# The maximum over the keys as a ScalarE copy and three two-operand maxima, normalised rows on ScalarE, and new core orders in a two-layer attention and SSM kernel

## The chip, the cores and the metric

The kernel runs on one core of a Trainium2 chip. Its engines each work through their own instruction queue in order: TensorE (PE in the profile; PEld is its weight load), VectorE (DVE), ScalarE (ACT), GpSimd (POOL), and SyncE (SP), whose queue issues the DMAs here. Semaphores let one queue wait for another. The metric is the device time of one execution in microseconds; before the change it was 403.94 us (median of three runs, 403.01 to 404.91).

## The reference

Two kinds of layer alternate, A, B, A, B, each added to its input after a layer norm. x has 2048 rows of 512 bfloat16 values.

```python
def _A_ref(x, wqkv, wo):            # H = 32 heads of Dh = 16; W, dil = 8, 2
    qkv = (x @ wqkv).reshape(B, S, 3, H, Dh) ...
    idx = pos[:, None] - off[None, :]            # 8 keys: the row itself and 2, 4, .. 14 rows back
    kg, vg = k[:, :, idx_c, :], v[:, :, idx_c, :]
    logits = jnp.einsum("bhsd,bhswd->bhsw", q, kg) * scale
    logits = jnp.where(mask, logits, -1e9)
    attn = softmax(logits, axis=-1)              # over the 8 keys
    o = jnp.einsum("bhsw,bhswd->bhsd", attn, vg)
    return o.reshape(B, S, D) @ wo

def _B_ref(u, ...):                 # a long convolution of each of the 512 columns with a kernel K
    ...                             # K from a sum over 128 complex modes; rfft, product, irfft
    return y + u * Dskip

x = x + _A_ref(layernorm(x), ...);  x = x + _B_ref(layernorm(x), ...)
x = x + _A_ref(layernorm(x), ...);  x = x + _B_ref(layernorm(x), ...)
```

A softmax is the same whatever is subtracted from all eight logits of a row, so the maximum need not be exact.

## The kernel before

The program is one stream of five stages: generation of the convolution kernels together with the front of attention layer 0 (up to about 108 us of the span), the core of attention layer 0 (to about 190 us), the first convolution as a chain of DFT matmuls together with the front of layer 1 (to about 266 us), the core of attention layer 1 (to about 356 us), and the second convolution (to the end). Inside a stage the order of every engine's queue is written by hand: a string of letters is walked, and each letter issues the instructions of one step. An engine takes its own instructions of these steps in the order of the string, so that a letter's place decides what stands ahead of it in each queue.

The rows are split so that row `16p + a` lies on partition `p` in block `a`; a core handles 16 blocks `a`, four of them to a group `q`. The steps of a core (`LayerA.core`) and their letters:

- `q`, `v` (lines 390 to 408): projections for the queries of one group and a quarter of the features, and for the values of one block. Four matmuls on PE, then an evacuation of PSUM by ACT. The last value blocks of even and of odd number start a DMA that shifts values between partitions.
- `m` (line 342): the products of queries and keys for one group and a quarter of the features, one DVE instruction of 128x4096; there are two buffers for them, so the second next `m` waits until PE has read the first.
- `l` (lines 350, 354): PE sums these products over the 16 features of a head, into the logits `L` of the group, 128x1024 float32 in PSUM. For the first two groups of a core `L` is laid out as (head, block) by key by row, for the other two as row by block by key by head.
- `x` (`mx`, line 414): DVE takes the maximum over the eight keys, from PSUM, as one `tensor_reduce` with 1024 elements in and 128 out, bfloat16.
- `e` (`sub_exp`, lines 425, 426): PE subtracts the maximum within PSUM with a negated identity matrix, then ACT takes the exponential.
- `r`, `n`, `T`: PE sums the exponentials, ACT forms the reciprocal by Ln and Exp, DVE multiplies (lines 445, 448), and for the first two groups PE and ACT turn the weights to rows (`T`).
- `P` (line 467): DVE multiplies the weights of one block with its eight value rows, 128x4096, into `pav`, of which there are two buffers.
- `S`, `V` (lines 482 to 494): PE sums `pav` over the keys and turns it, into the PSUM tile `po`, of which there is one; ACT evacuates it to `oT`. `S` and `V` take the blocks in the order in which `P` made them.
- `O` (lines 501 to 510): PE adds x and projects with `wo`; ACT writes `x_sb`, for blocks below 12 with the row sum, and squares it for the second sum.
- `b`, `d`, then `a` or `f`: the statistics of four blocks, and the normalised input of the convolution, one block of 128x512 at a time, on DVE (`a`, line 197) or on ACT (`f`, line 195). Both letters take the next block from one list of twelve; core 0 does eight of them there and leaves the others to POOL.
- Core 0 also holds work of the convolution to come: `0` and `2` to `5` make a table of sines on POOL and ACT, `1` and `6` issue loads, `8` and `9` add a row, `A` to `H` copy parts of the kernel to `k_perm` (line 1450; `B`, `C`, `E` on ACT, the others on DVE), `w` loads a matrix.

After core 0 the string `ORDER0` begins with `KD KA KA KA KD`: first DFT matmuls of the convolution kernels (line 802), their PSUM evacuated by DVE (`D`) or ACT (`A`) on line 791. After core 1 `ORDER1` begins with the same step for the normalised rows, so that it needs all twelve blocks and the last four.

Two lines set memory that the change touches. In layer 0 a tile `gap` keeps room free ahead of the work tiles:

```python
            if l == 0:
                wk.tile([P, 1680], BF16, name="gap", bufs=1)
```

Of the kernel before, what the change touches and what calls it, by code (L numbers as in the profile page):

```python
# [11 lines left out]
ALU = mybir.AluOpType  # L12
AX = mybir.AxisListType
PSUM = bass.MemoryType.PSUM
F32 = mybir.dt.float32
BF16 = mybir.dt.bfloat16
# [4 lines left out]
P = 128  # L21
# [4 lines left out]
W = 8  # L26
# [23 lines left out]
zUUUkkzkUztKkKtkkTUpexUUKUEkUkeUkUKpKUokxkpxpKUkUxxkqUKEpxoqkkUpUUxopXXXKQpZxxZZ  # L50
"""
ORDER0 = """
KD KA KA KA KD KA KD KA KD KA KD kA KA kD KA KD UA KD UA UA UD KA kA kD kA UD
UA UD UA kD kA kD u UD u u UA m m m UA u u UD u UA m kD UA kD UA m
m u UA u m kA u kD u m kD u kD kA kA yA m YA m yD u yA u m m m
u u yA m m u YA m yA w000D yD yA YD yA w010D YA yD yA
"""
LATE0 = "a s t g r b m"
ORDERF = """
yA h00 YA h01 v100A v110D h10 a0 z12A p0 z11A n0D h11 w001A w011A S a1 p1 T0 E01A z13A E00D n1G H2  # L60
P02 a2 P00 Q00 p2 T1 E10D E11D P01 P11 P12 n2D H3 a3 P13 T2 P10 E20D E21D P03 p3 P21 P22 n3D
P23 T3 E30D E31A P20 x1
"""
ORDER1 = """
UA UD UA UD UA UA UD UA UD UD u u m m u u m m UA u UA UD m UA u u
UD UA u m m u u m m u YD m u YA YA m u yD m yA u u m m u w001A
m m yA yA w000D YA yD yA YD w011D yA yD w010D yA yD yA v101A v103D v113A v102D v112D v111D v110A v100A
"""

CORE0 = """  # L70
vmvvvlmqlxmvvvemlvqrlmqvnTmlvxqqlmevlrvmmvvvvnPllPqxmSqTeO0mPlVrP15SOS2PnOPVPOSml4qOOlb3mV78lPPC
SOdxS6eOrPSPPOSnwaOPSBPOSaOS9bOfAPdbFPOtVftEGDSaafaOH
"""
CORE1 = """
0m1l2ml3mvvqlmvlvqmxmqvlqqvemllvmrqvlnmTmqxqlmvvelvvvvmPvPqvrlnlTqSmOSxmPqlPeSPOmSOSlOPrlSOqPSPO
SnmPOOlbxSOPePVbPrdSnPdfOVfaOPwSfPOSfOSbafOPdfaSttfaOa
"""
ROWS0 = (0, 2, 1, 3, 4, 5, 6, 7, 8, 9, 10, 11, 12, 13, 14, 15)
ROWS1 = (0, 2, 1, 3, 4, 5, 6, 7, 8, 9, 10, 11, 12, 13, 14, 15)
# [120 lines left out]
class LayerA:  # L200
# [158 lines left out]
    def core(self, x_sb, u, lnp, order, ev, nprod=0):  # L359

        tc, nc, lnst, l = self.tc, self.nc, self.lnst, self.layer
        ident, nident = self.c["ident"], self.c["nident"]
        scale = float(DH) ** -0.5
        xnT, ncol = self.xnT, self.ncol
        if self.ps_l is None:
            self.open_logits()
        st, linit, mult, lsum = self.st, self.linit, self.mult, self.lsum

        with ExitStack() as c2:
# [6 lines left out]
                self.load_wo(big)  # L376
            wk = c2.enter_context(tc.tile_pool(name=f"a{l}_wk", bufs=2, reuse_waits="tile"))
            if l == 0:
                wk.tile([P, 1680], BF16, name="gap", bufs=1)
            self.prp = c2.enter_context(tc.tile_pool(name=f"a{l}_prod", bufs=2, reuse_waits="tile"))  # L380
            pavp = c2.enter_context(tc.tile_pool(name=f"a{l}_pav", bufs=2, reuse_waits="tile"))
            ps_q = c2.enter_context(tc.tile_pool(name=f"a{l}_ps_q", bufs=2, space=PSUM))
# [27 lines left out]
            def mx(q):  # L410
                L = st[q]["L"]
                m = wk.tile([P, P], BF16, name="mx", bufs=1)[:]
                st[q]["mx"] = m if q < ncol else m.rearrange("p (a h) -> p a h", h=H)
                nc.vector.tensor_reduce(st[q]["mx"], L[:].rearrange("c w p -> c p w" if q < ncol else "p a w h -> p a h w"), AX.X, ALU.max)

            def sub_exp(q):
                L, m = st[q]["L"], st[q]["mx"]
# [120 lines left out]
            def calls(f, *args):  # L538
                return [lambda a=a: f(*a) for a in args]

            def logit(f):
                def g(q, ft):
                    if ft == 0:
                        linit(q)
                    f(q, ft)
                return g
# [5 lines left out]
                m=calls(mult, *qft[nprod:]), l=calls(logit(lsum), *qft[nprod:]),  # L552
                q=calls(q_proj, *qft[len(self.qT) * NDT:]), v=calls(v_proj, *((a,) for a in VROWS)),
                x=calls(mx, *blocks), e=calls(sub_exp, *blocks), r=calls(recip, *blocks), n=calls(norm_p, *blocks), T=calls(turn, *blocks[:ncol]),
                P=calls(pv_mult, *rows), O=calls(out_proj, *rows[:15]), t=calls(x_stats, (12,), (13,)),
                b=calls(u_begin, (0, 4, "act", "pool"), (4, 8, "act", "act"), (8, 12, "act", "act")),
# [1023 lines left out]
```

## Time and profile before

| | before |
|---|---|
| median of three runs | 403.94 us (403.01 to 404.91) |
| span of the profiled execution | 402.6 us, so 1.3 us of the median lie around it |
| busy DVE, PE, ACT, POOL | 95%, 81%, 80%, 15% of the span |
| maximum over the keys (line 414) | 8 instructions, 9.7 us on DVE |
| normalised rows in the cores, on DVE | 13 instructions, 5.1 us (line 197) |
| normalised rows in the cores, on ACT | 11 instructions, 8.9 us (line 195) |

A page of the profile gives the busy time of each engine, the chain of work that ended last, and groups of instructions with their mean duration. Further views are drawn from the same trace: busy time by stretches of the span, the instructions of one engine in order of time, and groups within a stretch. All times are of one execution; "start, duration" pairs of neighbouring instructions overlap a little on one engine, so that the distance from start to start, the step, is what an instruction costs its queue.

### The profile page before, as it was taken

How to read it: one execution, taken by the hardware profiler on the slowest of the kernel's cores; microseconds unless marked ns; L12 is line 12 of the kernel's file. 1: busy time of each engine (PE TensorE's matmuls, PEld its weight loads, DVE VectorE, ACT ScalarE, POOL GpSimd, SP SyncE). 2: the span in 40 equal slices, each digit the busy share in tenths (PEclk: the TensorE clock that was granted, in tenths of full speed). 3: DMA queues.
4: the chain of work that ended last, by engine and by line, in shares of the span. 5: the costliest groups of instructions: out<-in, count | busy, mean ns of one | idle time of the engine just before them, and what ended most of it. 6: DMA issues, size and time to landing. Idle time of an engine off the chain costs nothing.

```text
span 402.6 us, 14781 instructions
## 1 busy us (share of the span) xinstructions
PE 328.0 (81%) x6527; PEld 230.3 (57%) x6527; DVE 383.5 (95%) x460; ACT 321.8 (80%) x557; POOL 59.1 (15%) x75
## 2 busy tenths in 40 slices
PE   3000059999999989999998889999999998997895
PEld 2000026657735656756987888543456666566885
DVE  6999999999999999999999998979899999989994
ACT  7999888898656578988999987674666677989974
POOL 9402400000199500200600000100000001000000
PEclk9999997999999999999999999999999999999999
DMA  7952711115013875259236685730063019504606
GB/s 219 395 143 37 81 52 50 44 27 117 3 43 76 214 210 160 55 173 384 93 112 232 228 285 166 280 114 2 0 170 94 3 39 383 161 2 134 186 14 202
DMA packets 62323, 54.17 MB, mean 135 GB/s; under 512 B 33869, under 2 KB 50738, under 8 KB 60978
## 3 DMA queue, kind: packets, MB, share of 16 engines
q1 hardware_dynamic: 62250, 53.22, 43.5%
q8 instruction: 51, 0.84, 0.9%
q14 instruction: 14, 0.11, 0.1%
q10 hardware_dynamic: 8, 0.00, 0.0%
HBM read 30.15 MB, written 13.24 MB: 108 GB/s over the span
## 4 chain that ended last, share of the span: by engine, by line
PE 36%; DVE 31%; ACT 17%; issue 8%; DMA 5%; SPq 2%; POOL 1%; DVEq 0%; ACTq 0%; POOLq 0%
DVE pav L467 11%; PE pq L398 6%; PE pk L1268 5%; ACT a1s L791 5%; PE pp L1206 4%; DVE t L847 3%; PE pq L223 3%; DVE prod L342 3%; PE pp L282 3%; PE L L350 2%; ACT ub L860 2%; DVE B_t L1110 2%; DVE sq_z L1085 2%; DMA v_ext<-v_ext 2%; DMA kf_ring<-kf_dram 2%
## 5 line engine op out<-in xcount | busy, mean ns | idle before, releaser
L467 DVE TENSOR_TENSOR pav<-attn,v_ext 128x4096 bf16<-128x4096 bf16 (+1 forms) x34 | 72.4, 2168 | 0.4 <-DMA v_ext<-v_ext 0.3
L342 DVE TENSOR_TENSOR prod<-qT,kT_ext 128x4096 bf16<-128x4096 bf16 x29 | 67.0, 2341 | 1.4 <-PE L L350 0.9
L1196 PE MATMUL pt<-ident,x_blk 128*128 128x128 bf16 x64 | 5.9, 241 | 42.8 <-DVE x_blk L197 38.6
L1110 DVE TENSOR_TENSOR A_t<-A_t,pow_t 128x1024 bf16<-128x1024 bf16 (+4 forms) x46 | 38.3, 870 | 0.3
L492 PEld LDWEIGHTS <-pav 64*128 64x128 bf16 x1664 | 26.2, 95 | 13.5 <-DVE pav L467 8.6
L503 PE MATMUL pq<-wop,oT 128*128 128x512 bf16 x128 | 32.9, 379 | 0.7 <-ACT oT L494 0.7
L860 ACT CAST ub<-pb 128x1024 bf16<-128x1024 f32 x32 | 32.1, 1079 | 1.2 <-PE pb L809 1.2
L492 PE MATMUL po<-ident,pav 64*128 64x64 bf16 x1664 | 29.3, 190 | 4.2 <-DVE pav L467 3.2
L400 ACT CAST v_ext<-pq 128x512 bf16<-128x512 f32 x32 | 18.8, 586 | 16.2 <-PE pq L398 16.2
L809 PE MATMUL pb<-a1s,w_sb 128*128 128x64 bf16 x768 | 27.4, 193 | 5.0 <-ACT a1s L791 1.7
L398 PE MATMUL pq<-wv,xnT 128*128 128x512 bf16 x128 | 30.6, 380 | 0.0
L1206 PE MATMUL pp<-xnT,kT_ext 128*128 128x512 bf16 x96 | 27.1, 411 | 4.3 <-ACT kT_ext L1211 2.3
L1196 PEld LDWEIGHTS <-x_blk 128*128 128x128 bf16 x64 | 4.6, 107 | 44.8 <-DVE x_blk L197 38.8
L809 PEld LDWEIGHTS <-w_sb 128*128 128x128 bf16 x768 | 24.9, 98 | 7.2 <-issue 5.2
L791 ACT CAST a1s<-pb 128x1024 bf16<-128x1024 f32 x29 | 28.2, 1059 | 0.8 <-PE pb L802 0.8
L1268 PEld LDWEIGHTS <-A_t 128*64 128x64 bf16 (+1 forms) x512 | 22.9, 107 | 4.5 <-DVE B_t L1110 0.3
L1268 PE MATMUL pk<-B_t,A_t 128*64 128x84 bf16 (+1 forms) x512 | 24.6, 206 | 0.0
L791 DVE CAST a1s<-pb 128x1024 bf16<-128x1024 f32 x19 | 22.6, 1217 | 1.4 <-PE pb L802 1.3
L223 PE MATMUL pq<-xnT,kT_ext 128*128 128x512 bf16 x96 | 23.9, 380 | 0.0
L225 ACT CAST qT<-pq 128x512 bf16<-128x512 f32 x24 | 14.1, 586 | 9.3 <-PE pq L223 9.2
L509 ACT ACTIVATE x_sb<-pq 128x512 bf16<-128x512 f32 x24 | 14.3, 594 | 8.7 <-PE pq L503 8.7
L398 PEld LDWEIGHTS <-xnT 128*128 128x128 bf16 x128 | 11.6, 98 | 15.3 <-issue 3.0
(259 smaller groups left out, 897.0 us busy)
## 6 DMA issues: line engine op xcount, KB each, us to landing
w_sb<-w_dram SPq DMA_DIRECT2D x8, 1024.0 KB, 7.8
w_dram<-xnT SPq DMA_DIRECT2D x1, 4096.0 KB
kf_ring<-kf_dram SPq DMA_DIRECT2D x13, 256.0 KB, 4.8
kf_ring<-kf_dram SPq DMA_DIRECT2D x26, 128.0 KB, 4.3
v_ext<-v_ext SPq DMA_DIRECT2D x4, 784.0 KB, 6.6
x_blk<-in_A_x_dram SPq DMA_DIRECT2D x4, 512.0 KB, 4.1
kT_ext<-in_A_wqkv_dram SPq DMA_DIRECT2D x4, 512.0 KB, 9.2
x_sb<-in_A_x_dram SPq DMA_DIRECT2D x4, 512.0 KB, 5.3
```

The source lines that it names most:

```text
L223: nc.tensor.matmul(pq[:], lhsT=self.wqk[:, dt, ft * P:(ft + 1) * P], rhs=self.xnT[:, dt, q * 512:(q + 1) * 512], start=(dt == 0), stop=(dt ...
L342: nc.vector.tensor_tensor(pr, self.qT[q][:, ft].unsqueeze(1).to_broadcast([P, W, 4, P]), kap, ALU.mult)
L398: nc.tensor.matmul(pp[:], lhsT=xnT[:, dt, a * P:(a + 1) * P], rhs=wv[:, dt, :], start=(dt == 0), stop=(dt == NDT - 1))
L467: nc.vector.tensor_tensor(pv[:, i], attn[:, n % 4].unsqueeze(2).to_broadcast([P, W, DH // parts, H]), vap, ALU.mult)
L492: nc.tensor.matmul(po[:, h, 0, i * nt + ft, :], lhsT=pvf[rows, i, w, ft * P:(ft + 1) * P], rhs=ident[rows, rows], start=(w == 0 and ft + i ...
L503: nc.tensor.matmul(pw[:], lhsT=oT[:, ftp, :], rhs=self.wo[:, ftp, :], start=False, stop=(ftp == NDT - 1))
L791: (self.nc.scalar.copy if eng == "act" else self.nc.vector.tensor_copy)(dst, src)
L809: nc.tensor.matmul(p2[:, j, :], lhsT=self.w2[:, ec * EC + j, :], rhs=a1s[:, ec * EC + j, :], start=True, stop=True)
L860: nc.scalar.copy(ub[:], p2)
L1110: return lambda: nc.vector.tensor_tensor(*args)
L1206: nc.tensor.matmul(pps[kind, b, ft][:], lhsT=la.wqk[:, dt, c:c + P], rhs=la.xnT[:, dt, b * 512:(b + 1) * 512], start=(dt == 0), stop=(dt = ...
L1268: nc.tensor.matmul(o, lhsT=lhs, rhs=Bt[:, ri, c * CH + ql].rearrange("p b g -> p (b g)"), start=(not half and j % 4 == 0 and ri == 0), sto ...
```

## The change

The maximum becomes four instructions: ACT copies `L` from PSUM to a bfloat16 tile `lc` in SBUF, and DVE takes maxima of halves, of 4 keys with 4 (512 elements), of 2 with 2 (256) and of 1 with 1 (128), each on what the one ahead of it wrote. In layer 0 `lc` takes its room from `gap`; in layer 1 it gets a pool of its own on the other side of the memory, where the front's tiles have been closed. The strings of both cores are new; those of the other stages only have their lines broken elsewhere. In core 0 all eight normalised rows are `f` (they were three `f` and five `a`), in core 1 ten are `f` and two `a` (they were seven and five). All other letters occur as often as before.

```diff
 CORE0 = """
-vmvvvlmqlxmvvvemlvqrlmqvnTmlvxqqlmevlrvmmvvvvnPllPqxmSqTeO0mPlVrP15SOS2PnOPVPOSml4qOOlb3mV78lPPC
-SOdxS6eOrPSPPOSnwaOPSBPOSaOS9bOfAPdbFPOtVftEGDSaafaOH
+vvmm0vlxvvlemmvvrlvqqnvlTmqlqmmlxvvlevvrmmnvvvlqPTlSPmxqOVeqm15qll2PPmS4OOSPP3l78m6rVPOSCbOOPnVP
+BlxSPOOdSefwPSrfOPnSOPSfPOSfPOSbOAdffVb9fPODSHGfttEFO
 """
 CORE1 = """
-0m1l2ml3mvvqlmvlvqmxmqvlqqvemllvmrqvlnmTmqxqlmvvelvvvvmPvPqvrlnlTqSmOSxmPqlPeSPOmSOSlOPrlSOqPSPO
-SnmPOOlbxSOPePVbPrdSnPdfOVfaOPwSfPOSfOSbafOPdfaSttfaOa
+0mqq2mlm13lqlvvvmlvmmxvvllqevvmrmnqllqTqqmmlmxvvvvvvvvlPPqmlmeqlSmxrqSqnTPOOSePSPPOSOlPSbOOSPdfr
+flmmSffnPPOOllxSbOPVdPeSrffnPOVOSOPPSOfSwbfPOSdffaattO
 """
...
-                wk.tile([P, 1680], BF16, name="gap", bufs=1)
+                wk.tile([P, 1680 - W * P], BF16, name="gap", bufs=1)
+            lcp = c2.enter_context(tc.tile_pool(name="a1_lc", bufs=1, side="right", reuse_waits="tile")) if l else wk
...
                 st[q]["mx"] = m if q < ncol else m.rearrange("p (a h) -> p a h", h=H)
-                nc.vector.tensor_reduce(st[q]["mx"], L[:].rearrange("c w p -> c p w" if q < ncol else "p a w h -> p a h w"), AX.X, ALU.max)
+                lc = lcp.tile([P, W * P], BF16, name="lc", bufs=1)[:]
+                lc = lc.rearrange("c (w p) -> c w p", w=W) if q < ncol else lc.rearrange("p (a w h) -> p a w h", a=4, w=W)
+                nc.scalar.copy(lc, L[:])
+                for n in (4, 2, 1):
+                    lo, hi = (lc[:, 0:n], lc[:, n:2 * n]) if q < ncol else (lc[:, :, 0:n, :], lc[:, :, n:2 * n, :])
+                    one = st[q]["mx"].unsqueeze(1 if q < ncol else 2)
+                    nc.vector.tensor_tensor(lo if n > 1 else one, lo, hi, ALU.max)
```

More of the change, by code (lines that the diff above doesn't have):

```diff
@@ L52 @@
 ORDER0 = """
[L53 to L56, printed above, removed]
+KD KA KA KA KD KA KD KA KD KA KD kA KA kD KA KD UA KD UA UA UD KA kA kD kA UD UA UD UA kD kA kD u UD
+u u UA m m m UA u u UD u UA m kD UA kD UA m m u UA u m kA u kD u m kD u kD kA kA yA m YA m yD u yA u
+m m m u u yA m m u YA m yA w000D yD yA YD yA w010D YA yD yA
 """
@@ L60 @@
 yA h00 YA h01 v100A v110D h10 a0 z12A p0 z11A n0D h11 w001A w011A S a1 p1 T0 E01A z13A E00D n1G H2
-P02 a2 P00 Q00 p2 T1 E10D E11D P01 P11 P12 n2D H3 a3 P13 T2 P10 E20D E21D P03 p3 P21 P22 n3D
-P23 T3 E30D E31A P20 x1
+P02 a2 P00 Q00 p2 T1 E10D E11D P01 P11 P12 n2D H3 a3 P13 T2 P10 E20D E21D P03 p3 P21 P22 n3D P23 T3
+E30D E31A P20 x1
 """
 ORDER1 = """
-UA UD UA UD UA UA UD UA UD UD u u m m u u m m UA u UA UD m UA u u
-UD UA u m m u u m m u YD m u YA YA m u yD m yA u u m m u w001A
-m m yA yA w000D YA yD yA YD w011D yA yD w010D yA yD yA v101A v103D v113A v102D v112D v111D v110A v100A
+UA UD UA UD UA UA UD UA UD UD u u m m u u m m UA u UA UD m UA u u UD UA u m m u u m m u YD m u YA YA
+m u yD m yA u u m m u w001A m m yA yA w000D YA yD yA YD w011D yA yD w010D yA yD yA v101A v103D v113A
+v102D v112D v111D v110A v100A
 """
 CORE0 = """
-vmvvvlmqlxmvvvemlvqrlmqvnTmlvxqqlmevlrvmmvvvvnPllPqxmSqTeO0mPlVrP15SOS2PnOPVPOSml4qOOlb3mV78lPPC
-SOdxS6eOrPSPPOSnwaOPSBPOSaOS9bOfAPdbFPOtVftEGDSaafaOH
+vvmm0vlxvvlemmvvrlvqqnvlTmqlqmmlxvvlevvrmmnvvvlqPTlSPmxqOVeqm15qll2PPmS4OOSPP3l78m6rVPOSCbOOPnVP
+BlxSPOOdSefwPSrfOPnSOPSfPOSfPOSbOAdffVb9fPODSHGfttEFO
 """
 CORE1 = """
-0m1l2ml3mvvqlmvlvqmxmqvlqqvemllvmrqvlnmTmqxqlmvvelvvvvmPvPqvrlnlTqSmOSxmPqlPeSPOmSOSlOPrlSOqPSPO
-SnmPOOlbxSOPePVbPrdSnPdfOVfaOPwSfPOSfOSbafOPdfaSttfaOa
+0mqq2mlm13lqlvvvmlvmmxvvllqevvmrmnqllqTqqmmlmxvvvvvvvvlPPqmlmeqlSmxrqSqnTPOOSePSPPOSOlPSbOOSPdfr
+flmmSffnPPOOllxSbOPVdPeSrffnPOVOSOPPSOfSwbfPOSdffaattO
 """
```

## The prediction, as put down before the changed kernel had run

> **What bounds the kernel now.** I read the page first: it gives the span and the busy time of each engine.
>
> ```profile
> span 402.6 us, 14781 instructions
> ...
> PE 328.0 (81%) x6527; PEld 230.3 (57%) x6527; DVE 383.5 (95%) x460; ACT 321.8 (80%) x557; POOL 59.1 (15%) x75
> ```
>
> DVE is the fullest engine, but a share over five stages says little, so the next view is busy time by stage (bounds, length, then busy us of PE, PEld, DVE, ACT, POOL): core 0, first convolution, core 1, second convolution, and three stretches inside the cores.
>
> ```profile
> 108.30:190.50 82.20, 78.15 (x1495) 48.25 (x1493) 81.55 (x64) 61.55 (x124) 29.77 (x17) 1.00 0.53 157
> 190.50:265.80 75.30, 69.69 (x1689) 59.36 (x1690) 71.83 (x116) 66.59 (x85) 8.10 (x11) 1.00 0.59 204
> 265.80:356.50 90.70, 87.39 (x1576) 50.15 (x1573) 87.84 (x77) 63.56 (x135) 1.02 (x1) 1.00 0.30 96
> ...
> 167.30:191.10 23.80, 22.42 (x568) 14.63 (x568) 23.38 (x31) 20.45 (x48) 0.00 (x0) 1.00 0.67 237
> 265.80:291.00 25.20, 24.65 (x165) 9.92 (x162) 23.26 (x19) 14.89 (x26) 0.00 (x0) 1.00 0.02 7
> ...
> 351.05:356.50 5.45, 4.80 (x52) 2.19 (x50) 5.22 (x18) 4.84 (x11) 0.00 (x0) 1.00 0.05 16
> ```
>
> In core 0 DVE idles 0.65 of 82.2 us: whatever leaves its queue there should shorten the stage, until another engine sets the pace. ACT has 20.6 us free in core 0 and 27.1 in core 1, but only 3.35 in the last 23.8 us of core 0. In core 1 DVE idles 2.9 us. The groups of DVE within core 1 show on what (last column):
>
> ```profile
> L342 DVE TENSOR_TENSOR prod<-qT,kT_ext 128x4096 bf16<-128x4096 bf16 x16 | 36.2, 2286 | 1.3 <-PE L L350 0.9 <-DVE kT_ext L295 0.2
> L467 DVE TENSOR_TENSOR pav<-attn,v_ext 128x4096 bf16<-128x4096 bf16 (+1 forms) x17 | 36.1, 2160 | 0.4 <-DMA v_ext<-v_ext 0.3
> ```
>
> The chain of waits at the end of core 0 tells who receives the time saved there:
>
> ```profile
> 191.11 0.75 ACT a1s L791
> ...
> 197.94 5.49 ACT a1s L791 x6
> ```
>
> The first convolution begins as a queue of ACT evacuations. A gain of core 0 counts only as far as ACT comes free earlier than 191.11; DVE alone being early is worth nothing there.
>
> **The maximum.** What goes is one reduction for each group of rows, eight in all; what comes on DVE is three dependent maxima of 512, 256 and 128 elements. DVE in order of time:
>
> ```profile
> 18.43 0.42 DVE L1110 TENSOR_TENSOR B_t<-B_t,cm_t 128x512 bf16<-128x512 bf16 x1
> 18.77 0.69 DVE L1082 SCALAR_TENSOR_TENSOR sq_z<-sq_z 128x512 f32<-128x512 f32 x1
> ...
> 27.87 0.28 DVE L1110 TENSOR_TENSOR A_t<-A_t,pow_t 128x256 bf16<-128x256 bf16 x1
> 28.18 0.29 DVE L1110 TENSOR_TENSOR A_t<-A_t,A_t 128x256 bf16<-128x256 bf16 x1
> ...
> 167.32 1.21 DVE L414 TENSOR_REDUCE mx<-L 128x128 bf16<-128x1024 f32 x1
> 168.46 2.27 DVE L467 TENSOR_TENSOR pav<-attn,v_ext 128x4096 bf16<-128x4096 bf16 x1
> ...
> 175.66 0.40 DVE L197 TENSOR_SCALAR xnT<-x_sb,ln_rstd,ln_nb 128x512 bf16<-128x512 bf16 x1
> 175.98 2.27 DVE L467 TENSOR_TENSOR pav<-attn,v_ext 128x4096 bf16<-128x4096 bf16 x1
> ```
>
> The reduction costs its queue 1.14 us (167.32 to 168.46). A follower that is independent starts about 0.08 before the record ends (18.43+0.42 against 18.77), one that reads the result 0.03 after it (27.87+0.28 against 28.18). No row shows a bfloat16 maximum; the nearest are these two-operand instructions, which do multiply, add and subtract at one rate, so I price it as they are: 0.42+0.03, then 0.285+0.03, then 128 elements, by the same slope 0.215, less 0.07 of overlap with an independent follower: 0.92. Saved: 0.22 each, 0.88 in each core. Bounds: if the three did not wait for each other, 0.34+0.20+0.14 = 0.68, saving 0.46 each; if maxima ran like float32 instructions of the same size (18.77: 0.69 at 512, so 0.42 and 0.28 for the halves, again with 0.03, 0.03 and less 0.07), 1.38, a loss of 0.24 each. I take the dependent bfloat16 price.
>
> The Trainium skill, "VectorE: DVE Perf Modes", section "The DRAIN you can't avoid", speaks against splitting: no operation starts until the one ahead has emptied the pipe, so that its rules ask for fewer operations. The rows disagree with the first half (18.77 starts 0.08 before 18.43+0.42 is over). By that rule the reduction would cost its whole 1.21 and the three 0.42+0.28+0.215, a saving of 0.29 each, 2.3 in all against 1.8 by the rows.
>
> On ACT comes a 1024-element copy from PSUM. The exponential reads the same tile in the same shape:
>
> ```profile
> L426 ACT ACTIVATE ex<-L 128x1024 bf16<-128x1024 f32 x8 | 8.2, 1026 | 1.3 <-PE L L425 1.3
> ```
>
> less 0.09 of overlap, 0.93 each, 3.7 in each core. It lies ahead of the maximum, so it must be hidden: in both new strings one to three products or `P` stand on DVE between the last `m` of a group and its `x`, 2.2 us each, against PE's sums, this copy, and at most an evacuation ahead of it. I take no wait; without that cover each group would pay up to 0.93. What queues behind a copy that waits are the evacuations that free PE's two projection buffers.
>
> **The rows.** Five rows in core 0 and three in core 1 leave DVE: 0.32 each (175.66 to 175.98). On ACT they cost 0.71 (188.83 to 189.54), from its own tail in order of time:
>
> ```profile
> 187.41 1.03 ACT L1450 COPY k_perm<-k_rl 128x1024 bf16<-128x1024 bf16 x1
> 188.35 0.58 ACT L494 CAST oT<-po 128x512 bf16<-128x512 f32 x1
> 188.83 0.82 ACT L195 ACTIVATE xnT<-x_sb,ln_nb,ln_rstd 128x512 bf16<-128x512 bf16 x1
> 189.54 0.57 ACT L507 CAST x_sb<-pq 128x512 bf16<-128x512 f32 x1
> 190.54 0.59 ACT L507 CAST x_sb<-pq 128x512 bf16<-128x512 f32 x1 [0.42 <-PE pq L503]
> 191.11 1.01 ACT L791 CAST a1s<-pb 128x1024 bf16<-128x1024 f32 x1
> ```
>
> **The end of core 0.** The last `P` and what follows it on DVE:
>
> ```profile
> 186.05 1.22 DVE L467 TENSOR_TENSOR pav<-attn,v_ext 128x2048 bf16<-128x2048 bf16 x1
> 187.18 1.28 DVE L138 BATCH_NORM_STATS2 ln_bn<-x_sb 128x6 f32<-128x512 bf16 x2
> 188.38 0.75 DVE L1450 COPY k_perm<-k_rl 128x1024 bf16<-128x1024 bf16 x2
> 189.04 1.06 DVE L197 TENSOR_SCALAR xnT<-x_sb,ln_rstd,ln_nb 128x512 bf16<-128x512 bf16 x3
> ```
>
> It ends at 187.27. Ahead of it go four maxima (0.88), the first two `a` (0.64) and the copy `F`, which moves behind it (half of 188.38 to 189.04, 0.33): 1.85, so it ends at 185.42. From there ACT's path is PE's sum and the wait to the evacuation (187.27 to 188.35, 1.08), the evacuation 0.48, a row 0.71, the copy `E`, which now stands here, 0.94, and the two last `x_sb` 0.5 and 0.57: 4.28, so 189.70. ACT's work gives another bound. The last `x` starts three maxima earlier, 167.32-0.66 = 166.66; behind it ACT had 20.45 and now has 20.45+5x0.71 (rows)-0.94 (`B`, moved ahead)+0.48 (one evacuation moved behind) = 23.54, so 190.20 if its copy ends only then. It can end sooner, since three `P` lie between that group's last `m` and its `x`. Between 189.7 and 190.2 I take 189.9: **core 0 gives 1.2 us**.
>
> The moved DMA steps keep their order among themselves in SP's queue (value shifts, x, first kernel load, four stores of the sines, second load, matrix), and the sines come earlier, so nothing waits longer behind them. Only `8` moves ahead of its load's other work: it now stands before the last `m` and a `P`, about 157.5 instead of 162.64. SP's queue shows the issues of that load, and the view of its tile how long they take to land:
>
> ```profile
> 142.78 12.49 SPq L1373 DMA_DIRECT2D k_rl<-kd_dram  x17
> ```
>
> ```profile
> DMA to landing us min/median/max: 1.9/3.5/7.1
> ```
>
> The last lands near 155.27+3.5 = 158.8, but `8` reads only the row that an earlier issue brought: nothing, at most 1.3.
>
> **The end of core 1.** Ahead of its last `P` go four maxima (0.88) and two `a` (0.64): 1.5. The 0.9 us for L350 should go, since `l5` moves ahead of two projections and `e0` in PE's queue; late next is `n0`, which needs the reciprocal and now stands one `m` sooner after its `x`. The 0.3 for the value shift goes too, since all `v` now stand before the first `P`. I take half of 1.2: **core 1 gives 2.1 us**. Behind the last `P` lie the same PE sum, projection, statistics and scaling; one `a` less among DVE's 5.22 of 5.45 us shortens nothing there, PE and ACT cover it.
>
> **Sum.** 1.2+2.1 = 3.3 off the span of 402.6; the median lies 1.3 above that span, and I take that to stay: 403.9-3.3 = **400.6**. Both convolutions follow unchanged.
>
> **Rivals.** *More is saved.* The maxima cost 0.68 and all of core 1's idle time goes: core 1 gives 1.84+0.64+1.2 = 3.7, core 0 no more than ACT allows, 1.4: 398.8. For it: the strings are made for it; against: the dependent row.
>
> *PE takes over.* It is busy 24.65 of 25.2 us in the front of core 1. If its pace holds there, core 1 keeps the later three maxima and two rows, 1.3; if core 0's PE takes half of its gain, 0.6: 402.0.
>
> *ACT's queue paces the tail of core 0 (slower).* There is one `po`: PE cannot sum a block before ACT has emptied it, and now rows, `B`, `E` and copies stand between evacuations. If ACT's 3.35 us of waiting for PE stay, it comes free at 166.66+23.54+3.35 = 193.55, 2.4 late. It decides once more than 0.9 of these waits remain. With core 1's gain, 404.2; if ten rows there cost the 2.1 too, 406.3. For it: ACT's 20.45 of 23.8; against: the longer queue itself fills those waits.
>
> *Maxima at the float32 rate* (the change does not do what it says): core 0 loses 0.4 (0.96 more against 0.97 less ahead of the last `P`, then 4.28 for the 3.84 from 187.27 to 191.11), core 1 gains 0.3: 404.0.
>
> **How the numbers follow.** Forecast 0.45 (its own range 399.3 to 402.0); more saved 0.12; PE 0.18; ACT in core 0 alone 0.07; ACT in both 0.13; float32 rate 0.05. Half a per cent, 2.0 us, is about what a measurement of this kernel can tell from no change: faster is below 401.9. That takes 0.39 of the forecast, 0.12, and half of PE's 0.18: 0.60. Slower, above 406.0: most of ACT in both, 0.13. The rest, 0.27, is the same. Eight in ten: down to 398.3, the case of more saved less half a us, and up to 405.0, between the two cases of ACT, which leaves out most of the worse.
>
> **What would show it.** Step by step: the three maxima sum to 0.92 from start to start, and ACT's copies take 1.03; the last `P` of core 0 ends near 185.4 and the first ACT a1s starts near 189.9; the last `P` of core 1 ends about 3.3 earlier than 351.05, and DVE's 0.9 for L350 is gone. I am wrong if DVE waits for ACT's copy ahead of the maxima, if ACT a1s starts after 191.1, or if DVE's idle time in either core grows by more than 2 us.

## The result and the profile after

The changed kernel takes 407.93 us (median of four runs, 406.62 to 409.29) against 403.48 for the kernel before in the same series: ratio 1.0098, 95% interval 1.0069 to 1.0127. It is slower, where 400.6 was forecast. The page of the changed kernel begins:

```profile
span 406.0 us, 14747 instructions
...
PE 323.3 (80%) x6483; PEld 230.4 (57%) x6527; DVE 381.2 (94%) x468; ACT 333.3 (82%) x573; POOL 64.0 (16%) x75
```

DVE has 2.3 us less to do (383.5 before), about half of the 4.3 that the prediction takes off it (eight maxima at 0.22 and eight rows at 0.32), and the span is 3.4 longer. The following places are read off the two traces; a core is counted from its first product (`m`) to the first a1s behind it, on ACT for core 0 and on DVE for core 1.

| | before | after | forecast |
|---|---|---|---|
| core 0: first product | 110.77 | 110.70 | |
| core 0: last `P` ends | 187.27 | 189.83 | 185.42 |
| core 0: first a1s of ACT | 191.11 | 194.35 | 189.9 |
| length of core 0 | 80.34 | 83.65 | 79.1 |
| length of core 1 | 89.12 | 89.56 | 87.0 |

So core 0 lost 3.3 us where 1.2 were to be gained, and core 1 lost 0.4 where 2.1 were to be gained. Both convolutions pass this on to within 0.5 us. Busy time of the two cores of the changed kernel, then of the kernel before (bounds, length, then busy us of PE, PEld, DVE, ACT, POOL, granted clock, DMA share, GB/s):

```profile
110.70:194.35 83.65, 74.90 (x1456) 47.20 (x1470) 78.37 (x65) 66.91 (x132) 31.50 (x15) 1.00 0.53 160
271.96:361.52 89.56, 82.93 (x1586) 50.33 (x1604) 84.42 (x77) 66.81 (x140) 3.00 (x1) 1.00 0.30 100
```

```profile
110.77:191.11 80.34, 76.25 (x1469) 47.33 (x1468) 79.78 (x62) 60.46 (x122) 28.54 (x15) 1.00 0.55 164
268.56:357.68 89.12, 85.75 (x1604) 50.07 (x1604) 85.58 (x73) 61.84 (x133) 1.02 (x1) 1.00 0.30 97
```

The granted clock is 1.00 in all four, so PE's clock is not what makes this profile longer. In core 0 DVE now idles 83.65-78.37 = 5.3 us; before it was 80.34-79.78 = 0.6. What it waits for there, and in core 1 (time in total, times, longest):

```profile
DVE ln_nb L184 <- ACT ln_rstd L155: 1.9, 1, 1.9
DVE a1s L797 <- PE pb L808: 1.5, 1, 1.5
DVE pav L473 <- PE po L498: 0.6, 1, 0.6
DVE lc L420 <- ACT lc L416: 0.4, 1, 0.4
DVE k_perm L1456 <- issue: 0.2, 1, 0.2
...
DVE ln_nb L184 <- POOL ln_rstd L177: 0.9, 1, 0.9
DVE pav L473 <- PE po L498: 0.9, 1, 0.9
DVE ln_veps L171 <- ACT ln_junk L144: 0.3, 1, 0.3
```

None of these is the price of an operation. Followed upwards, core 0's waits begin at two places. The first is ACT's copy `C`, in ACT's order of time:

```profile
162.28 1.05 ACT L1456 COPY k_perm<-k_rl 128x1024 bf16<-128x1024 bf16 x1 [1.78 <-DVE pav L473]
```

The view names a `P` as the releaser, since one ended at 162.25, but `C` reads nothing that a `P` writes. `C` writes into the part of `k_perm` from which the sines are being stored, and its wait on the semaphore of the third of these stores ends as that store lands, at 162.06; in six of the experiments below the same wait is put down to `g_dram<-k_perm`, these stores. SP's queue in the changed kernel, then in the kernel before, shows when they are issued, and the matrix load `w` (4 MB, `w_sb<-w_dram`) behind them:

```profile
157.07 2.64 SPq L741 DMA_DIRECT2D g_dram<-k_perm  x4
159.76 1.05 SPq L1363 DMA_DIRECT2D k_rl<-kd_dram  x1
160.86 10.35 SPq L1379 DMA_DIRECT2D k_rl<-kd_dram  x17
171.32 2.24 SPq L597 DMA_DIRECT2D w_sb<-w_dram  x4
```

```profile
155.37 8.80 SPq L735 DMA_DIRECT2D g_dram<-k_perm  x4
164.23 0.61 SPq L1357 DMA_DIRECT2D k_rl<-kd_dram  x1
164.89 11.52 SPq L1373 DMA_DIRECT2D k_rl<-kd_dram  x17
176.51 1.96 SPq L591 DMA_DIRECT2D w_sb<-w_dram  x4
```

The last sine is done earlier now, so the four stores no longer take SP 8.8 us, and the matrix load starts 5.2 us earlier. The second place is PE, in order of time:

```profile
177.28 0.89 PE L498 MATMUL po<-ident,pav 64*128 64x64 bf16 x49 [0.16 <-ACT oT L500]
179.20 0.39 PE L498 MATMUL po<-ident,pav 64*128 64x64 bf16 x15 [1.04 <-issue]
...
182.94 0.75 PE L498 MATMUL po<-ident,pav 64*128 64x64 bf16 x39
185.40 0.54 PE L498 MATMUL po<-ident,pav 64*128 64x64 bf16 x25 [1.71 <-issue]
```

Twice PE stops in the middle of a sum `S` and waits for nothing that the profile shows. Then ACT's evacuation is late, behind it Ln and Exp of `b`, and DVE's `d` and the last `P` behind that (DVE in order of time):

```profile
184.63 0.43 DVE L1456 COPY k_perm<-k_rl 128x1024 bf16<-128x1024 bf16 x1 [0.21 <-issue]
186.94 0.16 DVE L184 SCALAR_TENSOR_TENSOR ln_nb<-ln_s,ln_rstd 128x4 f32<-128x4 f32 x1 [1.88 <-ACT ln_rstd L155]
...
187.49 2.34 DVE L473 TENSOR_TENSOR pav<-attn,v_ext 128x2048 bf16<-128x2048 bf16 x2
```

What PE waits for is read from the DMA queue with the kind "instruction", of the page:

```profile
q8 instruction: 51, 0.84, 0.9%
```

51 packets of 16 KB. From the first stop to the second PE issues 30 instructions of the rest of that `S` (a matmul and its weight load count two), 10 of an `O`, 128 of an `S`, 10 of an `O` and 78 of the next `S`: 256, and 16,384 bytes over 256 is 64 each. The packets' own records: one moves from 176.68 to 177.72 and PE goes on at 179.20; the next from 182.89 to 183.91 and PE goes on at 185.40, 1.48 and 1.49 us behind each. So PE stands until a block of instructions has come. Why the blocks come late had to be tried.

### The profile page after: what moved, and what is told of

Same layout as the page of the kernel before. It is cut to its first block, busy times and chain, and to the rows that moved or that the text cites. A ratio compares the mean times of both kernels' runs of the same rounds, so it can differ in the third digit from the quotient of the medians.

```text
span 406.0 us, 14747 instructions
## 1 busy us (share of the span) xinstructions
PE 323.3 (80%) x6483; PEld 230.4 (57%) x6527; DVE 381.2 (94%) x468; ACT 333.3 (82%) x573; POOL 64.0 (16%) x75
## 4 chain that ended last, share of the span: by engine, by line
PE 36%; DVE 17%; ACT 11%; issue 6%; POOLq 1%; DMA 1%; SPq 0%; DVEq 0%; ACTq 0%
PE pq L398 5%; PE pq L222 4%; PE pq L509 4%; PE po L498 4%; DVE prod L341 4%; DVE t L853 4%; PE pp L281 3%; DVE pav L473 2%; PE pb L815 2%; ACT ub L866 2%; ACT a1s L797 2%; PE pb L808 2%; DVE a1s L797 2%; ACT ln_junk L144 1%; ACT x_sb L515 1%
## 5 line engine op out<-in xcount | busy, mean ns | idle before, releaser
L341 DVE TENSOR_TENSOR prod<-qT,kT_ext 128x4096 bf16<-128x4096 bf16 x29 | 66.0, 2312 | 0.6 <-DVE kT_ext L294 0.3
L509 PE MATMUL pq<-wop,oT 128*128 128x512 bf16 x123 | 31.8, 379 | 3.0 <-issue 2.1
L1212 PE MATMUL pp<-xnT,kT_ext 128*128 128x512 bf16 x88 | 26.0, 414 | 4.9 <-ACT kT_ext L1217 2.3
L398 PE MATMUL pq<-wv,xnT 128*128 128x512 bf16 x122 | 29.5, 379 | 0.3
L222 PE MATMUL pq<-xnT,kT_ext 128*128 128x512 bf16 x89 | 23.0, 379 | 0.5 <-issue 0.2
L500 ACT CAST oT<-po 128x512 bf16<-128x512 f32 x26 | 15.0, 577 | 7.0 <-PE po L498 6.9
L177 POOL TENSOR_TENSOR ln_rstd<-ln_rstd,ln_mh 128x4 f32<-128x4 f32 x2 | 6.0, 3006 | 92.4 <-DVE ln_rstd L176 92.4
```

The source lines that it names most:

```text
L222: nc.tensor.matmul(pq[:], lhsT=self.wqk[:, dt, ft * P:(ft + 1) * P], rhs=self.xnT[:, dt, q * 512:(q + 1) * 512], start=(dt == 0), stop=(dt ...
L341: nc.vector.tensor_tensor(pr, self.qT[q][:, ft].unsqueeze(1).to_broadcast([P, W, 4, P]), kap, ALU.mult)
L398: nc.tensor.matmul(pp[:], lhsT=xnT[:, dt, a * P:(a + 1) * P], rhs=wv[:, dt, :], start=(dt == 0), stop=(dt == NDT - 1))
L509: nc.tensor.matmul(pw[:], lhsT=oT[:, ftp, :], rhs=self.wo[:, ftp, :], start=False, stop=(ftp == NDT - 1))
L1212: nc.tensor.matmul(pps[kind, b, ft][:], lhsT=la.wqk[:, dt, c:c + P], rhs=la.xnT[:, dt, b * 512:(b + 1) * 512], start=(dt == 0), stop=(dt = ...
```

## Experiments

Each kernel ran in several rounds beside the kernel before; the ratio is to that kernel, with its 95% interval. The changed kernel stands at 1.0098.

**Order or maxima.** e1 has both old strings with the new maxima, e2 both new strings with the old reduction, e3 the changed kernel with core 0's old string.

```diff
 e1: CORE0, CORE1 as before                  e3: CORE0 alone as before
 e2:
-                nc.scalar.copy(lc, L[:])
-                for n in (4, 2, 1): ...
+                nc.vector.tensor_reduce(st[q]["mx"], L[:].rearrange(...), AX.X, ALU.max)
```

> The maxima with ScalarE's copy as in the changed kernel, both core orders as in the kernel before. Theory N (the new order of core 0 is what loses): no slower than before, 402.5 to 404.0: the six maxima that run beside idle POOL give 0.22 each, 1.3, and the two of core 0 that run beside POOL's tensor_scalar cost 0.2 and 0.6 more than the reduction. Theory M (maxima and copies lose): 406 or more, with DVE waiting for ACT's copies.

> Both new orders, the maximum a reduction from PSUM as before and no copy on ACT. Theory N: slower than before, 406.5 to 409; in core 0 PE again stands still inside a sum of S for over 1 us with nothing it waits for, while the matrix load moves, and DVE waits for Ln and Exp. Theory M: 403.5 or less.

> The changed kernel with the order of core 0 as before; core 1 keeps its new order. Theory N: some 3.3 us less than the changed kernel, 404.0 to 405.0, since core 1 lost only 0.4. Theory M: 407 to 408.5, since the eight maxima and copies are all still there.

Measured: e1 420.8 us (1.0407, 1.0376 to 1.0439), e2 408.15 (1.0109, 1.0077 to 1.0141), e3 412.04 (1.0204, 1.0170 to 1.0239). Theory N holds for e2 and falls for e1 and e3: each part of the change loses by itself. In the old strings the maxima cost 16.6 us, and DVE's waits in e1 tell where:

```profile
DVE lc L420 <- ACT lc L416: 16.0, 7, 5.3
```

A reduction reads `L` as soon as PE is done; the copy stands in ACT's queue behind its evacuations. The old strings put `x` right behind the last `m`, so DVE waits; the new ones put products or `P` between. That is what they buy, and e2 against the changed kernel shows the price: with the reduction the new orders alone lose as much as the whole change, so the maxima gain nothing that shows. In e2 the wait of `C` is longer still, and its releaser is named (first ACT, then DVE, in order of time):

```profile
164.01 1.05 ACT L1450 COPY k_perm<-k_rl 128x1024 bf16<-128x1024 bf16 x1 [2.69 <-DMA g_dram<-k_perm]
```

```profile
174.39 4.49 DVE L467 TENSOR_TENSOR pav<-attn,v_ext 128x4096 bf16<-128x4096 bf16 x2 [2.45 <-PE po L492]
```

Behind `C` stands an evacuation of `po`; PE then waits 2.52 us for it, and DVE 2.45 for PE, whose granted clock was 0.51 from 169.3 to 172.7, just behind its wait. PE's stops are no matter of the new order alone: in e1 and e3, whose core 0 has the old string, the load starts within 1 us of its old time (176.99 and 177.43), the sums come later, and PE stops for up to 1.89 and 1.62 us.

**One wait at a time in core 0.** From here on the edits are to the changed kernel's CORE0 string.

```diff
 e4 (w late)      -...OOdSefwPSrf...bOAdffVb9fPOD...      +...OOdSefPSrf...bOAwdffVb9fPOD...
 e5 (C late)      -...VPOSCbOOPnVPBlxSPOO...               +...VPOSbOOPnVPBlxCSPOO...
 e6 (rows to DVE) -...efwPSrfOPnSOPSfPO...Vb9fPODSHGfttEFO +...eawPSraOPnSOPSaPO...Vb9PODSHGttaaEFO
 e7 (d late)      -...bOAdffVb9fPODSHG...                  +...bOAVb9PdffOfDSHG...
 e8 (V for S)     -...PnSOPSfPOSfPOSbOA...                 +...PnVOPVfPOVfPOVbOA...
```

> The changed kernel with the matrix load of core 0 (w) issued five P later, behind the statistics of the third block. Theory F (PE's stalls of 1.04 and 1.71 us are instruction blocks that arrive late behind the load's packets): the stalls inside S near 178 and 184 fall below 0.5 us each, and core 0 ends 1 to 2.5 us earlier, so 405.4 to 407. Rival (the stalls come from the dense row of S's alone, whatever the DMA queues carry): they stay and the time stays within 0.5 us of the changed kernel's.

> The changed kernel with the k_perm copy C of core 0 issued behind ACT's copy for the last maximum, so that the stores of the sines have landed when ACT comes to it. Theory W (this copy stops ACT, and what stands behind it is late): the waits of 1.78 us of ACT, 1.34 us of PE and 0.38 us of DVE near 162 to 168 are gone, and core 0 ends 0.4 to 1.5 us earlier: 406.4 to 407.5. Rival (the late end of core 0 is made behind 176 alone): the waits go and the time stays within 0.4 us of the changed kernel's.

> The changed kernel with five of the eight rows of core 0 on DVE, as many as before, two of them behind the last P. Theory A (ACT's queue sets the end of core 0): 3.5 us less work for ACT and 1.6 more for DVE; ACT's first a1s starts 1.5 to 2.5 us earlier, 405.4 to 406.4. Rival (PE's late sums and DVE's wait for Ln and Exp set it): within 0.5 us of the changed kernel, or later by the three rows of 0.32 ahead of the last P.

> The changed kernel with DVE's step d of the second four blocks behind the last P of core 0 instead of ahead of it, and the two rows that read it behind it too. Theory D (DVE waits for ACT's Ln and Exp in d, and the last P behind it is late): the wait of 1.9 us is gone, the last P ends 1.5 to 2 us earlier, and core 0 ends 0.7 to 1.9 us earlier: 406.0 to 407.2. Rival (ACT's queue sets the end): the last P is earlier, ACT's first a1s is not, time within 0.4 us.

> The changed kernel with four sums of core 0 as V (64 matmul and weight instructions in 1.95 us) in place of S (128 in 1.11 us). Theory F (PE runs out of instructions in the row of S's, since one block of them holds two S's and comes about every 4 us): PE's stalls of 1.04 and 1.71 us near 178 and 184 shrink to 0.5 or less; PE works 3.4 us more where it had them; time between 1.0 less and 0.5 more than the changed kernel's. Rival (the stalls do not depend on how many instructions PE issues): they stay, and PE's longer sums come on top: 1.5 to 3 us slower than the changed kernel.

Measured: e4 409.15 (1.0116, 1.0089 to 1.0143), e5 406.57 (1.0087, 1.0064 to 1.0111), e6 407.05 (1.0076, 1.0047 to 1.0104), e7 408.02 (1.0105, 1.0090 to 1.0120), e8 407.67 (1.0094, 1.0081 to 1.0108). All intervals overlap that of the changed kernel, and none reaches 1: no wait alone is the whole loss. e4 tells nothing on its question, since SP issued the load at 171.63 as ever: a letter further on in the string does not delay a DMA when nothing ahead of it in SP's queue waits. In e5 the waits of `C` and of DVE for its copy are gone and core 0's profile is 1.0 shorter, but PE stops 1.62 us at 179.04. In e7 DVE's wait for Ln and Exp is gone, its last `P` ends at 187.08, and ACT's first a1s comes at 194.12: the rows that moved behind it fill ACT's end. In e8 no stop of PE over 0.21 us is left between 174 and 192, so they do depend on how many instructions PE issues, but the longer `V` take their place (DVE waits 0.50 and 0.57 for them).

**Where the matrix load lies.** e9 is e5 with `w` ahead of the second kernel load, so that it really moves earlier. e10 has one `V` for `S` near 149 us, to move the borders of the blocks. e15 takes the kernel before, and moves nothing in it but `w`; the second kernel load is thereby issued 1.5 us later. e13 is e5 with the load held until DVE has written one element of each quarter of its tile, just ahead of the last `P`.

```diff
 e9   -...l78m6rVP...OOdSefwPS...      +...l78mw6rVP...OOdSefPS...       (and C late)
 e10  -...qll2PPmS4OOS...              +...qll2PPmV4OOS...
 e15  -...CSOdxS6eOr...OSnwaOP...      +...CSOdxSw6eOr...OSnaOP...       (CORE0 of before)
 e13  -...OOdSefwPS...Vb9fPODS...      +...OOdSefPS...Vb9fwPODS...       (and C late)
+        if held:
+            self.nc.vector.memset(w2[:, 0:P * P].rearrange("p (c x) -> p c x", c=4)[:, :, 0:1], 0.0)
         for c in range(4):
             self.nc.sync.dma_start(self.w2[:, c * 32:(c + 1) * 32, :], ...)
```

> The kernel of e5 (copy C late) with the matrix load w of core 0 ahead of the second kernel load in SP's queue, so that its 4 MB move near 160 to 172 and not 172 to 184. Theory F2 (an instruction block of PE is fetched late while this load fills the DMA engines): the stall of 1.62 us inside S near 179 is gone (under 0.5), and any stall over 0.8 us lies between 160 and 173; time 405.0 to 406.3. Rival (the stalls go with the place of the blocks in the row of S's, not with the load): stalls of over 1 us stay near 178 to 186, time as e5, 406.2 to 407.2.

> The changed kernel with one sum of core 0 near 149 us as V in place of S: 64 instructions fewer for PE ahead of the stalls, so that the borders between blocks of 256 instructions move 64 instructions on in all later work. Theory F (a block that begins early in an S after a row of S's comes too late): the stalls of 1.04 and 1.71 us inside the S's near 178 and 184 move to other matmuls and shrink below 0.8 us each, time 406.3 to 407.5. Rival (the stalls belong to these S's): they stay after 49 and 39 matmuls, and the time is the changed kernel's or up to 0.8 us more, since V takes PE 0.84 longer.

> The kernel before with nothing changed but its matrix load of core 0, which goes ahead of the second kernel load in SP's queue and so moves near 165 to 176 and not 178 to 188, under sums that follow each other faster. Theory F2: a stall of PE of 0.8 us or more between 165 and 178, and core 0 ends 0.5 to 2 us later: 404.4 to 406.0. Rival (the load's place is without effect): 403.3 to 404.2, as the kernel before.

> The kernel of e5 (C late) with the matrix load of core 0 held back until DVE has written one element of each quarter of its tile, just ahead of the last P, so that its 4 MB move from about 187 on, behind the S's (in e4 the letter alone had moved and the load had not). Theory F2 (PE's instruction blocks are late under this load): no stall over 0.6 us inside PE's sums between 165 and 188, core 0 ends 0.7 to 1.7 us earlier than in e5, 405.0 to 406.0. Rival (the stalls belong to the row of S's, or they hide nothing): stalls over 1 us stay or the time stays at 406.2 to 407.2.

Measured: e9 407.88 (1.0101, 1.0070 to 1.0131), e10 410.94 (1.0168, 1.0145 to 1.0192), e15 410.22 (1.0164, 1.0133 to 1.0196), e13 405.33 (1.0043, 1.0020 to 1.0066). In e9 the stop near 179 is gone and a worse one of 3.11 us ends at 176.05, behind a block that moved from 173.26 to 174.74, as the load ended; it holds up the last group's weights, and the granted clock was 0.50 from 175.5 to 178.9, so the time is no better. Its place answers to F2, at the edge of what was expected; that it grew I had not foreseen. e10 is inconclusive: the stops moved (one of 1.11 us, now after 12 matmuls of an `S` at 183.40), but `C` waited 3.07 us and PE 2.90 behind it, and PE's clock was 0.50 from 167.2 to 170.6, which covers the rest.

e15 is the clearest. PE of the kernel before, with its load moved from 176.5 to 163.4 in SP's queue, in order of time:

```profile
172.32 0.24 PE L492 MATMUL po<-ident,pav 64*128 64x64 bf16 x5 [1.22 <-issue]
...
175.91 0.90 PE L492 MATMUL po<-ident,pav 64*128 64x64 bf16 x49
180.16 0.58 PE L492 MATMUL po<-ident,pav 64*128 64x64 bf16 x15 [3.35 <-issue]
```

Moving four DMAs, and no engine's work, costs 6.6 us. The block behind the second stop moved from 177.50 to 178.70, and PE went on 1.46 later. The size was far beyond the 0.5 to 2 us that I had expected. DVE also waits 0.95 us for the kernel load that is now behind `w`, and another effect is in it (granted clock third from the end, then DMA share):

```profile
172.00:176.00 4.00, 3.47 (x83) 2.02 (x86) 3.45 (x5) 2.47 (x6) 0.00 (x0) 1.00 1.01 417
176.00:180.00 4.00, 0.81 (x49) 0.69 (x48) 2.02 (x1) 1.41 (x4) 0.00 (x0) 0.88 0.56 104
180.00:184.00 4.00, 3.51 (x61) 2.09 (x63) 3.05 (x6) 2.48 (x5) 0.00 (x0) 0.50 0.12 31
```

Within the long stop PE's clock falls to half, and its next matmuls take about twice as long.

e13 is the converse: no load under the sums, and no stop. Core 0 in time windows, and all that DVE waits for between 140 and 192:

```profile
109.89:190.12 80.23, 75.04 (x1456) 47.09 (x1470) 78.14 (x66) 66.67 (x131) 31.50 (x15) 1.00 0.45 132
```

```profile
DVE a1s L799 <- PE pb L810: 1.2, 1, 1.2
DVE k_perm L1458 <- issue: 0.2, 1, 0.2
```

Core 0 takes 80.23 us: 3.4 less than in the changed kernel, 0.1 less than before.

**Core 1, and the repairs together.** In e11 core 0 is wholly as before (order and reduction); core 1 has the maxima and the new string, with `d` of its first rows moved behind a product. e16 is e13 with this `d`, e17 the same with the load held two `P` less; e12 and e14 are e9 and e13 with five rows of core 0 on DVE and this `d`.

```diff
 CORE1 (e11, e12, e14, e16, e17)   -...SbOOSPdfrflmmSffnPP...   +...SbOOSPrlmdffmSffnPP...
 e17, CORE0                        -...SfPOSfPOSbOA...b9fwPOD   +...SfPOSfwPOSbOA...b9fPOD
```

> Core 0 as in the kernel before (order and reduction); core 1 with maxima and its new order, but its first step d behind a product, so that DVE doesn't wait 0.9 us for POOL's power. If core 0's new order makes nearly all of the loss and this wait is what takes core 1's saving: 402.7 to 403.7, as fast as the kernel before or up to 1 us faster. If core 1's order loses by itself elsewhere: 404 to 405.5.

> The changed kernel with four repairs at once: C late, w early, five rows of core 0 on DVE, and d of core 1 behind a product. If the repairs add up (1.4 for C, 1.0 for the stalls, 0.8 for the rows, 0.9 for d): 403.5 to 404.8, level with the kernel before. If one takes the place of another (the same end of core 0 is set by the last chain each time): 405.3 to 406.5.

> e13 with five rows of core 0 on DVE and with d of core 1 behind a product. If the three waits of core 0 (C, instruction blocks, rows on ACT) and the one of core 1 are what makes the changed kernel slower: 403.2 to 404.6, level with the kernel before. If the new order of core 0 loses by something else as well: 405 to 406.5.

> e13 (C late, matrix load of core 0 held until the last P; rows left on ACT) with d of core 1 behind a product. If the two repairs add up: 1.0 less than e13 against the kernel before, ratio 0.9995 to 1.003, 403.4 to 404.8. If DVE's 0.9 us in core 1 is taken by the next wait, as in e14: ratio 1.003 to 1.006.

> e16 with the matrix load held to two P earlier, from about 178. Theory F2: the load lies again under sums and one block is late, a stall of 0.5 to 1.5 us in S near 184, 0.5 to 1.5 us more than e16. Rival (the convolution gains from the earlier matrix, and PE has slack for the stall): up to 0.6 us less than e16.

Measured: e11 403.89 (1.0003, 0.9985 to 1.0021), e12 405.93 (1.0069, 1.0038 to 1.0100), e14 405.90 (1.0057, 1.0036 to 1.0078), e16 403.99 (1.0007, 0.9985 to 1.0029), e17 404.41 (1.0010, 0.9987 to 1.0032). e11 shows that core 1 loses nothing once `d` doesn't wait for POOL (its length there is 88.5), and with it that all the rest of the loss is core 0's. e16 is level with the kernel before: three repairs, none of which touches the maxima or the rows, take back the whole loss. In e12 a stop of 1.85 us at 174.10 remains. e14 differs from e16 in five rows of core 0 that are back on DVE, and is 1.9 us slower (its interval starts at 1.0036, that of e16 ends at 1.0029). How much of this the rows cost stays open: in the profiles core 0 has 0.5 of it (81.12 against 80.66) and core 1, whose string is the same, 1.8 (90.60 against 88.81), with a stop of PE of 1.26 us and half its clock from 335.7 to 339.1. e17's load (182 to 192) lies under the last sums and no stop over 0.2 us lies under it, so F2's 0.5 to 1.5 us were not seen. In the kernel before, too, the load lay under sums (DMA share 0.97 from 176 to 188) and PE stopped for 0.3 us at most: such a load does harm in some places and not wherever there are sums. No version beat the kernel before.

## Why the prediction was wrong

**The maxima: right away from POOL, wrong beside it.** 0.92 us from start to start was forecast; the four of core 1 and two of core 0 took 0.91 to 0.93. The copies took 1.01, as forecast, and DVE waited 0.4 for one of eight. But in core 0 up to the last `P` the four maxima took DVE as long as the reductions had. Groups of DVE there, after and before:

```profile
L341 DVE TENSOR_TENSOR prod<-qT,kT_ext 128x4096 bf16<-128x4096 bf16 x13 | 30.1, 2341 | 0.1
L420 DVE TENSOR_TENSOR lc<-lc 128x512 bf16<-128x512 bf16 x4 | 2.5, 623 | 0.4 <-ACT lc L416 0.4
L451 DVE TENSOR_TENSOR ex<-ex,rs 128x1024 bf16<-128x1024 bf16 x2 | 2.2, 1098 | 0.0
...
L420 DVE TENSOR_TENSOR lc<-lc 128x256 bf16<-128x256 bf16 x4 | 1.5, 385 | 0.1
...
L420 DVE TENSOR_TENSOR mx<-lc 128x128 bf16<-128x128 bf16 x4 | 0.9, 225 | 0.1
```

```profile
L342 DVE TENSOR_TENSOR prod<-qT,kT_ext 128x4096 bf16<-128x4096 bf16 x13 | 30.8, 2408 | 0.1
L414 DVE TENSOR_REDUCE mx<-L 128x128 bf16<-128x1024 f32 x4 | 4.8, 1209 | 0.0
...
L445 DVE TENSOR_TENSOR ex<-ex,rs 128x1024 bf16<-128x1024 bf16 x2 | 1.4, 678 | 0.0
```

2.5+1.5+0.9 = 4.9 against 4.8: the 0.88 of core 0 is not there. The groups of the first two `x` took 1.33 and 1.70, and both scalings `n` 1.10 where they had 0.68. The step that failed here is the price taken from the rows near 18 and 28 us, where POOL runs nothing: it asked how long such an instruction takes, and not what runs on POOL at its new place.

**The end of core 0: the step that failed.** "It ends at 185.42" took the old end of the last `P` less what DVE no longer does. It came at 189.83, 4.4 later. Of this, 0.38+0.58+0.21+1.88 = 3.05 are DVE's waits ahead of it, 0.21 of which the kernel before had too, and 1.3 are instructions beside POOL: 1.2 for the maxima (4.9 for 4x0.92) and 0.8 for the two `n`, less the 0.7 that the products took less; some 0.3 of the 4.4 is left without a place. I had priced every instruction and let DVE run through, though the new string changes what each one waits for.

**The moved DMAs: the sentence that was furthest off.** The clause "the sines come earlier, so nothing waits longer behind them" was true of SP's queue and beside the point. ACT comes to `C` 5.0 us earlier (160.5 instead of 165.48), but the store that `C` waits for is issued only 0.5 earlier (158.39 instead of 158.93), so that `C` waits for it to land (1.78 us; 2.69 in e2), and 4 MB that start 5.2 us earlier lie under other sums. e5 takes away the one and e13 both, and core 0 is back at 80.23; e15 puts the load under such sums in the kernel before and loses 6.6.

**The rows on ACT: right.** They took 0.70 to 0.72 each, and e16, with all eight on ACT, is not slower than e14, with three. Behind the last `P` ACT needed 194.35-189.83 = 4.5 us, as forecast (189.9-185.42).

**Core 1.** The 0.9 for the sums and the 0.3 for the value shift went, as forecast, and DVE has 1.2 us less to do (85.58 before, 84.42 now; 1.5 forecast). But new waits of 0.9 (POOL's power in `d`), 0.9 and 0.3 took their place. The second is again a stop of PE inside an `S`, 1.16 us up to 312.93, behind a block that moved at 310.35 just as the value shift's transfer ended (DMA share 0.99 from 306 to 308). No run moved that transfer, so the cause is argued; what such a stop costs shows in e16 and e17, which share e11's string of core 1: e16, with a stop of 0.98 us there, takes 88.81 us, e17, with none, 88.25. "Late next is `n0`" named the wrong one: `d` now stands one `P` behind its `b`. e11 moves it, and core 1 is 0.6 shorter than before in its profile; in the medians that is within what can be told.

**The rivals.** "ACT's queue paces the tail of core 0" came nearest in time (406.3 with core 1's gain gone; ACT free at 193.55, measured 194.35), with a chance of 0.13 where it had the gain of neither core. Its reason was not the one: in e6 three of the eight rows are left to ACT and core 0 is 0.7 shorter, while in e13 ACT has all eight and core 0 is 3.4 shorter. ACT was late because what it waited for was late. The range, up to 405.0, held no case in which a DMA's new place stops PE.

**Where the forecast 3.3 us went.** Even in e16, with those waits gone, nothing is gained: in core 0 the maxima give nothing beside POOL and DVE still waits 1.2 us for PE's first DFT matmuls, which in the new order stand behind all of core 0's sums; in core 1 a little is gained that the runs can't tell from nothing.

## What to carry to other kernels

When an order is rewritten by hand, price the waits as well as the work: for each step that moves, ask which transfer must have landed, and where each large transfer now lies, since a queue without waits of its own runs ahead of its letters. A stage with thousands of small matmuls needs a stream of instructions as well as of data; look where a multi-megabyte load falls in it. And before splitting an operation into cheaper ones, see which other engine's buffers and ports the old one didn't need: here an ACT copy that must be hidden and SBUF operands beside POOL.

## What the runs showed of the hardware

PE's instructions come by DMA in blocks of 256, and in all nineteen stops over 1 us that the profiles show between 108 and 364 us PE went on 1.31 to 1.57 us after the block's packet had moved. Each of these blocks moved while other transfers held the DMA share near 1.0 or just after they had ended; in e13, with a share of 0.01 to 0.03 from 172 to 184, PE shows no stop over 0.2 in core 0's sums there. The reverse does not hold: in e17 a block moved at 186.02 under a share of 1.0, and PE did not stop. What holds an instruction packet up was not tried.

In the stop of 3.35 us in e15 the granted clock fell to 0.50, and stayed there for 6.8 us (179.0 to 185.8). The Trainium skill, "TensorE: Matmul & The Clock Gate", Part 1, says that an idle window of about 3.4 us halves PE's clock. In these traces less was enough: the clock was 0.50 for 3.4 us behind a stop of 3.11 us in e9 and a wait of 2.90 in e10, and in e13 from 333.3 to 336.7, although PE was busy for 2.27 of the 3.4 us ahead of that. What PE must do to keep its clock no run here shows.

DVE lost about 0.4 us each of the eight times that a `TENSOR_SCALAR` of POOL (128x512) ended in core 0 of the changed kernel; DVE ran an instruction with two SBUF inputs each time. The maximum at 115.52 took 0.83 instead of 0.42 as POOL's ended at 116.08, the scaling at 121.25 took 1.10 instead of 0.68 as it ended at 121.81. A reduction from PSUM over such an end (115.59 to 116.80 in the kernel before, POOL's ending at 116.15) took its usual 1.21. The Trainium skill, "SBUF — State Buffer", section "Who interferes with whom", says that a DVE instruction with two SBUF inputs contends with a GpSimd instruction that reads SBUF, that a reduction never does, and that the ports which the two share are an exclusive lock. The traces fit: POOL is the one that waits longer. Its instruction of this shape took 0.69 us beside a reduction (at 127.57 in the kernel before) and up to 4.84 beside products, while the products inside that time took their usual 2.28.
